# Moving the DMAs that sum w3 w_out from the end of attention into the products of the second and third pair of rows

## The chip, the cores and the metric

The kernel runs on one core of one Trainium2 chip. The metric is the device time of one execution in microseconds; lower is better. The engines are TensorE (PE in the profile, with its weight loads as PEld), VectorE (DVE), ScalarE (ACT), GpSimd (POOL) and SyncE (SP). Here SP issues the plain DMAs; POOL issues the DMAs that accumulate into their target.

## The reference

Causal attention is followed by two feed-forward blocks. All arrays are float32, and the matmuls are done on a high and a low part of each operand, in three products.

```
attn = softmax(mask(q @ k.T / 8)) @ v           # 2 batches, 12 heads, 448 tokens, 64 per head
x    = attn as (896 tokens, 768)
ab   = (x @ w1) * (x @ w2)                      # w1, w2: 768 x 1024
h    = (ab @ w3) @ w_out                        # w3: 1024 x 1024, w_out: 1024 x 768
out  = relu(h @ w_in2)**2 @ w_out2              # w_in2: 768 x 2048, w_out2: 2048 x 768
```

## The kernel before

The kernel computes W = w3 w_out during attention, in gaps between attention's own matmuls, so that h = ab W is a single matrix product. W has 1024 rows, kept as 8 blocks of 128 rows. Each finished block is stored from the tile `wraw` into the DRAM tile `w_dram` (L588; the last block by L858).

The products x w1, x w2 and ab W are done in the manner of Strassen, with seven products of sums of blocks in place of eight. The products run in the order `SEVEN = "1265734"`, and each number has its own sum of blocks on either side. For ab W, products 1, 2 and 4 read blocks of `w_dram` itself, and products 5, 6, 3 and 7 read sums of its blocks. These sums are made by DMAs alone, in the DRAM tile `s_dram`, with one group of four sums for each pair of row blocks d (0 to 3). `w_sums(d)` first copies one block four times into `s_dram[d]` with one SP DMA of 768 KB (L914), and then accumulates three other blocks with POOL DMAs (L917) of 576, 576 and 192 KB. Each of the four DMAs needs the one before it. The fourth group also needs the last block of W, which is stored at the very end of attention.

After the last matmuls of attention the work is written by hand into a list, `prog`. Each entry names its engine with a cost, what it reads and writes, and optional predecessors (`after`). `prog.order()` plays the list through with the costs and gives every engine its order. An entry given as a predecessor only in `after` places the entry in that order; it makes no wait on the chip when no data goes between the two. TensorE's order is fixed by `plan`:

- four pairs of rows d = 0 to 3, each with 14 products of 9 matmuls with 448 columns. For each number of `SEVEN`, first the product with the pair of w1 and then the one with the pair of w2 (`("w2", m)` with m = 2d) is done;
- the products of ab W, called h products here, 36 matmuls for each number. The blocks of W come in two halves, i = 0 (groups d = 0 and 1) and i = 1 (groups d = 2 and 3), and each half is one load into a slot of `xs` (L970), one cast by ScalarE into the ring and one low half by VectorE (L820);
- the last two products, with w_in2 and w_out2, up to the end.

A block of w1 or w2 comes as 768 KB into one of two `raw` buffers (L187). ScalarE (L996) and VectorE (L1000, L1004) turn it into float32; SP's next load waits until L1004 has read the buffer. ScalarE casts it into one of 8 ring slots (L827), and VectorE makes the low half there (L820). The x blocks are made in the same manner: three of B21 in `xB`, and then T2, T1, T3 and T4 in tiles named `xT`. The `xT` tiles lie in memory that attention and `wraw` have used, so the first casts into them wait until the last store of `wraw` has landed. Each of ScalarE, VectorE, POOL and SP does its instructions strictly in order.

Before the change all four calls of `w_sums` stand in `prog` without a predecessor, ahead of everything of the products:

```
    for d in range(KF // 2):
        w_sums(d)
```

Of the kernel before, what the change touches and what calls it, by code (L numbers as in the profile page):

```python
# [122 lines left out]
def attention_moe_moe2(ctx: ExitStack, tc: tile.TileContext, qk, v, w1, w2, w3, w_out, w_in2, w_out2, out):  # L123
    nc = tc.nc
    NP_ALL, P, S2 = qk.shape
    S = S2 // 2
# [8 lines left out]
    KF = w1.shape[0]  # L135
# [37 lines left out]
    def mm(o, l, r, start, stop, **more):  # L173
        return nc.tensor.matmul(o, l, r, start=start, stop=stop, **more)  # L174
# [79 lines left out]
    def wide(u):  # L254
        return u[0] in ("H", "wout2")
# [27 lines left out]
    for u in units:  # L283
# [3 lines left out]
        else:  # L287
            nm, m = key
# [459 lines left out]
    prog = Program({"A": 700, "V": 100})  # L748
# [3 lines left out]
    def act(width, psum=False, strided=False):  # L752
        gap = 60 + 0.815 * width if psum else 75 + (0.96 if strided else 0.845) * width
        return {"A": (gap, gap + 105)}

    def dve(width, fast=False):
        gap = 70 + (0.52 if fast else 1.038) * width
        return {"V": (gap, gap + 85)}
# [7 lines left out]
    def pe(columns):  # L766
        return {"T": (columns * PE_ROW, columns * PE_ROW + 170)}
# [3 lines left out]
    def bank(i):  # L771
        if i not in banks:
            pool, tag = (pools["ps"], "mm") if i < 6 else (ps_w, "w")
            banks[i] = pool.tile([P, S], F32, tag=tag, name=f"bank{i}")
        return banks[i]
# [13 lines left out]
    def slot_of_block(of, n, k):  # L789

        if of == "x":
            return "x", n, k
        if of == "h":
            return XSLOTS[H_AT[n] + k]
        if n in ("T2", "T1", "T3"):
            return XSLOTS[("T2", "T1", "T3").index(n) * (KF // 2) + k]
        return "G", 2 * k, int(n in ("B21", "B22"))

    def part_of_slot(slot, r):
        kind, n, k = slot  # L800
        if kind == "x":
            return tiles["x", n][:, r, k]
        return g_tile("ab", n)[:, r, k * S:(k + 1) * S]

    def both_parts(slot):
        return [slot + (r,) for r in "hl"]
# [12 lines left out]
    def tt(out, x, y, what):  # L819
        return lambda e: engine_of[e].tensor_tensor(out(), x(), y(), op=what)  # L820
# [5 lines left out]
    def copy(out, x):  # L826
        return lambda e: engine_of[e].copy(out(), x()) if e == "A" else engine_of[e].tensor_copy(out(), x())  # L827
# [13 lines left out]
    def fs_at(i):  # L841
        return lambda: fs[:, i]

    def bank_at(i, width=S):
        return lambda: bank(i)[:, :width]
# [57 lines left out]

    S_AT = {"5": 0, "6": 1, "3": 2, "7": 3}

    def w_sums(d):
        a21, a22 = (w_dram[d, i, :, HN:] for i in range(2))
        a11, a12 = (w_dram[d, i, :, :HN] for i in range(2))
        last_row = [("wdram",)] * (d == KF // 2 - 1)

        def spread(x, n):
            return x.unsqueeze(1).to_broadcast([P, n, HN])

        prog.add({"S": (600, 4000)}, lambda e: nc.sync.dma_start(out=s_dram[d], in_=spread(a21, 4)),  # L914
                 last_row, [("sums", d)])
        for x, n0, n1 in ((a22, 0, 3), (a11, 1, 4), (a12, 2, 3)):
            prog.add({"P": (900, 5000)}, lambda e, x=x, n0=n0, n1=n1: nc.gpsimd.dma_start(  # L917
                out=s_dram[d][:, n0:n1], in_=spread(x, n1 - n0), accum_op=ALU.add),
                last_row + [("sums", d)], [("sums", d)])

    for d in range(KF // 2):
        w_sums(d)

# [117 lines left out]
    def ring_names(u):  # L1043
        k = slot_of[u]
        return [("ring", i, s) for i in ((k, k + 1) if wide(u) else (k,)) for s in "hl"]
# [3 lines left out]
    def take_bank():  # L1049
        return free_banks.pop(0)  # L1050

    def take_fs():
        return free_fs.pop(0)

    def out_of_bank(i, n):

        prog.add(act(S, True), copy(fs_at(n), bank_at(i)), [("bank", i)], [("fs", n)])
# [56 lines left out]
    def ab_places(of, n):  # L1114

        places.update(slot_of_block(of, n, k) for k in range(KH if of == "x" else KF // 2))
        for at in [x for x in ab_later if x[0] in places]:
            ab_later.remove(at)
            at[1]()
# [16 lines left out]
    def dummy(t, i, whole):  # L1136


        def run(e):
            if whole:  # L1140
                mm(bank(i), t[0][:, :P], xB["B11"][:, 0, 0], True, True)
            else:
                x = t[0][:, :P].bitcast(F32)
                mm(bank(i)[:, HN:], x, x[:, :S - HN], False, True, skip_group_check=True)

        return run

    def product(n, pair, unit, first_of_all):


        st = state.setdefault(pair, {})
        nm, m = pair
        of, out = ("h", g_out) if nm == "win2" else ("x", ab_out)
        t = hls[unit]
        chain = CHAIN[n]
        start = chain not in st
        if start:
            st[chain] = take_bank()
        i = st[chain]
        if n == "1":  # L1160
            j = st["b"] = take_bank()
            if written[j] < S:
                prog.add(pe(S if not written[j] else 2 * (S - HN)), dummy(t, j, not written[j]),
                         ring_names(unit)[:1] + [("x", "B11", 0, "h")], [("bank", j)])
            written[j] = S
        if start:
            written[i] = S
        slots = [slot_of_block(of, B_OF[n], k) for k in range(KH)]

        def run(e):  # L1170
            o = bank(i)
            if first_of_all:
                x = t[0][:, :P].bitcast(F32)
                mm(o[:, :PAUSE], x, x[:, :PAUSE], True, True)
            for k in range(KH):
                for s, r in ((0, 0), (0, 1), (1, 0)):
                    mm(o, t[s][:, k * P:(k + 1) * P], part_of_slot(slots[k], r),
                       start and k == 0 and (s, r) == (0, 0), k == KH - 1 and (s, r) == (1, 0),
                       skip_group_check=True)

        prog.add(pe(9 * S), run, ring_names(unit) + [x for slot in slots for x in both_parts(slot)]
                 + ([] if start else [("bank", i)]), [("bank", i)])
        if n == "1":
            prog.add(act(S, True), copy(bank_at(j), bank_at(i)), [("bank", i)], [("bank", j)])
        elif n in "65":
            st[n] = take_fs()
            out_of_bank(i, st[n])
        elif n in "73":
            r = st["5" if n == "7" else "6"]
            prog.add(dve(S), tt(fs_at(r), bank_at(i), fs_at(r), ALU.add), [("bank", i), ("fs", r)], [("fs", r)])  # L1190
            out(nm, m + (n == "7"), 0, r, None)
        else:
            out(nm, m + (n == "4"), 1, None, i)
        if n in "234":
            free_banks.append(i)
        if pair == ("w2", KF - 2):
            ab_places("x", B_OF[n])

    h_state = {}

# [120 lines left out]
    for at, (kind, what, which, used) in enumerate(plan):  # L1321
        for u in used:
            need_unit(u)
        if kind == "product":
            product(what, which, used[0], at == 0)
        elif kind == "h":
            h_step(what, *which, used[0])
        else:
            o_step(*what, which, used[0])
# [52 lines left out]
```

## Time and profile before

| | us |
|---|---|
| median of three runs | 546.79 (546.46 to 547.61) |
| profiled execution | 551.16 |
| its span | 549.4 |
| TensorE busy | 534.0 (97% of the span) |
| VectorE busy | 422.0 (77%) |
| ScalarE busy | 342.0 (62%) |
| POOL busy | 138.8 (25%) |

The shares are means over stages with different limits. Times in the trace are counted from the start of the span. Attention ends, and the products of the first pair of rows begin, at about 163 us; the h products begin at about 273 us.

### The profile page before, as it was taken

What the parts mean: (1) busy time and instruction counts of PE and PEld (TensorE: products, weight loads), DVE (VectorE), ACT (ScalarE), POOL (GpSimd) and SP (SyncE); (2) the same over time, 40 slices, a digit from 0 to 9 for tenths busy, and PEclk for the clock granted to TensorE, in tenths of its full rate; (3) what the DMA queues carried; (4) which work ended last, traced back from release to release, by engine and by line L of the source; (5) the groups of instructions that cost most, each with busy time, mean ns of one, the idle gap of its engine ahead of it and who ended that gap; (6) DMA issues with size and microseconds to landing.
All of it is one profiled execution on the core that took longest, in us unless ns stands there. A gap on an engine that the chain in (4) does not pass through costs nothing.

```text
span 549.4 us, 8338 instructions
## 1 busy us (share of the span) xinstructions
PE 534.0 (97%) x2977; PEld 475.7 (87%) x2977; DVE 422.0 (77%) x892; ACT 342.0 (62%) x748; POOL 138.8 (25%) x113
## 2 busy tenths in 40 slices
PE   7899989999997999999999999999999999999997
PEld 5658777888886999999999999999999999999997
DVE  4988788877777999999975899948677768776522
ACT  5787777777766665657565578926790479047800
POOL 3477776676941200000000039200010000000100
PEclk9999999999998999999999999999999999999999
DMA  8964544486889874335444311551624062403022
GB/s 294 338 206 142 159 134 170 151 241 161 213 209 278 207 216 154 134 115 140 119 114 145 119 55 58 172 173 59 203 85 172 1 194 94 173 0 116 0 110 92
DMA packets 25673, 81.27 MB, mean 148 GB/s; under 512 B 2272, under 2 KB 11744, under 8 KB 25632
## 3 DMA queue, kind: packets, MB, share of 16 engines
q1 hardware_dynamic: 21856, 75.24, 41.1%
q0 software_dynamic: 3776, 5.51, 6.4%
q8 instruction: 23, 0.38, 0.3%
q14 instruction: 18, 0.15, 0.1%
HBM read 74.84 MB, written 14.55 MB: 163 GB/s over the span
## 4 chain that ended last, share of the span: by engine, by line
PE 87%; ACT 5%; DVE 4%; DMA 2%; issue 1%; ACTq 0%; DVEq 0%
PE bank L174 68%; PE w L174 10%; PE s L174 4%; PE x L174 3%; PE pp L499 3%; ACT p L471 2%; DMA w_dram<-wraw 2%; ACT pt L510 1%; DVE p L464 1%; DVE xs L204 1%; ACT xs L198 1%; DMA qk<-in_qk 1%; DVE p L481 0%; DVE xs L820 0%; ACT hl_wout L193 0%
## 5 line engine op out<-in xcount | busy, mean ns | idle before, releaser
L174 PE MATMUL bank<-xT,ring 128*128 128x448 f32 x630 | 133.7, 368 | 0.0
L174 PEld LDWEIGHTS bank<-xT,ring 128*128 128x128 f32 x630 | 117.9, 188 | 10.9
L827 ACT CAST ring<-xs 128x384 fp32r<-128x384 f32 (+1 forms) x142 | 80.5, 581 | 75.0 <-PE bank L174 52.3
L174 PE MATMUL bank<-ring,g 128*128 128x384 f32 x672 | 117.2, 334 | 0.0
L174 PEld LDWEIGHTS bank<-ring,g 128*128 128x128 f32 x672 | 116.7, 188 | 0.1
L820 DVE TENSOR_TENSOR ring<-xs,ring 128x384 fp32r<-128x384 f32 (+1 forms) x142 | 91.3, 659 | 26.7 <-ACT ring L827 25.5
L481 POOL TENSOR_SCALAR p<-p,st 112x448 f32<-112x448 f32 (+1 forms) x84 | 97.4, 1292 | 45.0 <-DVE st L478 16.9
L174 PE MATMUL bank<-xB,ring 128*128 128x448 f32 x489 | 105.4, 371 | 3.1 <-DVE xB L820 1.8
L174 PEld LDWEIGHTS bank<-xB,ring 128*128 128x128 f32 x489 | 92.8, 190 | 12.5 <-DVE xB L820 2.1
L471 ACT ACTIVATE p<-p,st 112x448 f32<-112x448 f32 (+1 forms) x96 | 49.7, 529 | 27.6 <-DVE st L464 27.5
L820 POOL TENSOR_TENSOR g<-fs,g 128x448 fp32r<-128x448 f32 x5 | 12.1, 2434 | 162.7 <-ACT g L827 162.7
L820 DVE TENSOR_TENSOR acc<-bank,acc 128x384 f32<-128x384 f32 x42 | 21.4, 552 | 28.5 <-PE bank L174 28.3
L464 DVE CUSTOM_DVE_ANT_0 p<-s,mask 112x448 f32<-112x448 f32 (+1 forms) x96 | 36.5, 443 | 6.8 <-PE s L174 6.8
L174 PE MATMUL w<-hl_wout,w 128*128 128x384 f32 x192 | 36.2, 340 | 0.0
L820 POOL TENSOR_TENSOR xB<-fs,xB 128x448 fp32r<-128x448 f32 x3 | 3.8, 1271 | 126.2 <-ACT xB L827 126.2
L820 DVE TENSOR_TENSOR xs<-xs 128x384 f32<-128x384 f32 x64 | 34.4, 554 | 0.3
L827 ACT COPY fs<-bank 128x448 f32<-128x448 f32 x49 | 26.1, 533 | 13.5 <-PE bank L174 12.9
L174 PEld LDWEIGHTS w<-hl_wout,w 128*128 128x128 f32 x192 | 32.9, 188 | 1.3 <-issue 0.9
L174 PE MATMUL s<-qk 64*112 64x112 f32 (+3 forms) x192 | 28.5, 436 | 4.5 <-DMA qk<-in_qk 4.4
L499 PE MATMUL pp<-ident,p 112*112 112x112 f32 x240 | 27.4, 262 | 3.5 <-DVE st L464 2.7
L499 PEld LDWEIGHTS pp<-ident,p 112*112 112x112 f32 x240 | 23.6, 133 | 7.7 <-POOL p L481 3.1
L174 PE MATMUL bank<-gab,ring 128*128 128x448 f32 x144 | 30.1, 368 | 0.0
(89 smaller groups left out, 704.4 us busy)
## 6 DMA issues: line engine op xcount, KB each, us to landing
raw_wout<-in_w_out SPq DMA_DIRECT2D x24, 768.0 KB, 4.5
raw_w<-in_w SPq DMA_DIRECT2D x16, 768.0 KB, 6.0
raw_win<-in_w_in SPq DMA_DIRECT2D x16, 768.0 KB, 4.3
raw_w<-in_w SPq DMA_DIRECT2D x16, 512.0 KB, 4.0
qk<-in_qk SPq DMA_DIRECT2D x12, 448.0 KB, 5.3
s_dram<-w_dram POOLq DMA_DIRECT2D x8, 576.0 KB, 8.5
w_dram<-wraw SPq DMA_DIRECT2D x8, 384.0 KB, 6.2
s_dram<-w_dram SPq DMA_DIRECT2D x4, 768.0 KB, 6.9
```

The source lines that it names most:

```text
L174: return nc.tensor.matmul(o, l, r, start=start, stop=stop, **more)
L198: nc.scalar.activation(y, high.bitcast(F32), AF.Prelu, scale=2.0 ** -112, alpha=-2.0 ** 32)
L204: nc.vector.scalar_tensor_tensor(y.bitcast(U32), y.bitcast(U32), 3, low, op0=ALU.logical_shift_left, op1=ALU.bitwise_or)
L464: nc.vector.tensor_tensor_reduce(e, ps[j, i], mask[:, S - (i + 1) * CP:], QS, 3.0e38, ALU.add, ALU.min, st_t[p][:, 0, j, i:i + 1],)
L471: nc.scalar.activation(e, e, AF.Exp, bias=st_t[p][:, 0, j, i:i + 1], scale=-1.0, accum_out=st_t[p][:, 1, j, i:i + 1])
L481: engine.tensor_scalar(e, e, st[:, 3, i:i + 1], None, ALU.mult)
L499: nc.tensor.transpose(x[:CP, o:o + CP], pt[:, off[i] + c * CP:off[i] + (c + 1) * CP], ident[:CP, :CP],)
L510: nc.scalar.copy(pt_t[h][:, coff[PT[gi][0]]:coff[PT[gi][0]] + o], x[:CP, :o])
L820: return lambda e: engine_of[e].tensor_tensor(out(), x(), y(), op=what)
L827: return lambda e: engine_of[e].copy(out(), x()) if e == "A" else engine_of[e].tensor_copy(out(), x())
```

## The change

`w_sums` gets a predecessor, and its four calls move from the end of attention into the function that adds a product to `prog`. Groups 0 and 1 are added behind products 1 and 4 with w2 of the second pair of rows (m = 2), groups 2 and 3 behind the same products of the third pair (m = 4). Only the SP copy has the predecessor; the POOL DMAs follow it by their data. Nothing else is changed.

```diff
-    def w_sums(d):
+    def w_sums(d, behind):
...
         prog.add({"S": (600, 4000)}, lambda e: nc.sync.dma_start(out=s_dram[d], in_=spread(a21, 4)),
-                 last_row, [("sums", d)])
+                 last_row, [("sums", d)], after=[behind])
...
-    for d in range(KF // 2):
-        w_sums(d)
...
-        prog.add(pe(9 * S), run, ring_names(unit) + [x for slot in slots for x in both_parts(slot)]
+        at = prog.add(pe(9 * S), run, ring_names(unit) + [x for slot in slots for x in both_parts(slot)]
                  + ([] if start else [("bank", i)]), [("bank", i)])
...
         if pair == ("w2", KF - 2):
             ab_places("x", B_OF[n])
+        if nm == "w2" and 0 < m < KF - 2 and n in "14":
+            w_sums(m - 2 + int(n == "4"), at)
```

## Rows read from the trace of the kernel before

**Rows 1.** The chain that ended last: start us, us, what.
```profile
162.03 8.87 DMA w_dram<-wraw
...
172.51 373.13 PE bank L174 x1918
```
**Rows 2.** TensorE's timeline, 162 to 180 us; brackets: idle time before, and what ended it.
```profile
162.81 0.47 PE L174 MATMUL bank<-xB,ring 128*128 128x448 f32 x1
...
169.93 1.30 PE L174 MATMUL bank<-xB,ring 128*128 128x448 f32 x5 [1.77 <-DVE xB L820]
172.51 3.58 PE L174 MATMUL bank<-xB,ring 128*128 128x448 f32 x9 [1.28 <-ACT bank L827]
175.94 4.29 PE L174 MATMUL bank<-xT,ring 128*128 128x448 f32 x20
```
**Rows 3.** Windows: busy us of PE, PEld, DVE, ACT, POOL; granted clock; DMA share; GB/s.
```profile
172.50:176.00 3.50, 3.49 (x10) 3.12 (x11) 3.50 (x8) 3.50 (x8) 0.81 (x1) 0.53 1.12 255
...
217.00:243.00 26.00, 26.00 (x128) 23.61 (x127) 25.84 (x50) 14.72 (x28) 0.00 (x0) 1.00 0.40 130
```
**Rows 4.** Timelines of VectorE, then of ScalarE, 168 to 178 us.
```profile
168.78 0.56 DVE L1000 TENSOR_SCALAR raw_w<-raw_w 128x768 uint32<-128x768 uint32 x1 [3.97 <-DMA raw_w<-in_w]
169.26 1.16 DVE L820 TENSOR_TENSOR xB<-fs,xB 128x448 fp32r<-128x448 f32 x2
...
176.49 1.03 DVE L820 TENSOR_TENSOR ring<-xs,ring 128x384 fp32r<-128x384 f32 x2
...
171.00 1.03 ACT L827 CAST xT<-fs 128x448 fp32r<-128x448 f32 x2 [1.28 <-DMA w_dram<-wraw]
...
171.94 0.53 ACT L827 COPY bank<-bank 128x448 f32<-128x448 f32 x1
```
**Rows 5.** DMA issues and us to landing: issued at 159.9, 162.0, 103.2, 200 to 215 us.
```profile
raw_w<-in_w SPq DMA_DIRECT2D x1, 768.0 KB, 8.9
...
w_dram<-wraw SPq DMA_DIRECT2D x1, 384.0 KB, 8.9
...
w_dram<-wraw SPq DMA_DIRECT2D x1, 384.0 KB, 2.3
...
raw_w<-in_w SPq DMA_DIRECT2D x3, 768.0 KB, 4.1
```
**Rows 6.** TensorE's timeline: starts of the second, third, fourth pair; h product 6.
```profile
194.53 7.81 PE L174 MATMUL bank<-xB,ring 128*128 128x448 f32 x37
...
220.78 7.60 PE L174 MATMUL bank<-xB,ring 128*128 128x448 f32 x36
...
246.82 7.60 PE L174 MATMUL bank<-xB,ring 128*128 128x448 f32 x36
...
287.74 11.32 PE L174 MATMUL bank<-xB,ring 128*128 128x448 f32 x54
```
**Rows 7.** The sums: POOL's triggers (ns minimum, median, maximum; starts), then the page's DMA issues.
```profile
L917 POOL DMA_DIRECT2D s_dram<-w_dram x12: 807/1270/2476, 119.3 to 195.3; - x12
...
s_dram<-w_dram POOLq DMA_DIRECT2D x8, 576.0 KB, 8.5
...
s_dram<-w_dram SPq DMA_DIRECT2D x4, 768.0 KB, 6.9
```
**Rows 8.** A load of the third pair, its first reader; landing of the load of 172.3 us.
```profile
229.01 0.33 SPq L187 DMA_DIRECT2D raw_w<-in_w  x1
...
237.93 0.90 ACT L996 ACTIVATE xs<-raw_w 128x768 f32<-128x768 f32 x1
...
raw_w<-in_w SPq DMA_DIRECT2D x1, 768.0 KB, 11.1
```
**Rows 9.** h product 6, second half: load, cast; landing of the sum issued at 163.3 us.
```profile
259.80 0.36 SPq L970 DMA_DIRECT2D xs<-s_dram  x1
...
280.93 0.84 ACT L827 CAST ring<-xs 128x768 fp32r<-128x768 f32 x1
...
s_dram<-w_dram SPq DMA_DIRECT2D x1, 768.0 KB, 16.7
```

## The prediction

> **What bounds the kernel now.** I began with the chain of waits. Its last link is one unbroken run of 1,918 TensorE matmuls from 172.51 us to 545.65 us; the link ahead of it is the store of the last row of w3 w_out, 8.87 us from issue to landing [rows 1]. So from 172.51 us on TensorE sets the end, and a microsecond taken out ahead of that point, and not lost again behind it, comes off the end. The second view is TensorE's timeline where the products begin. The first product starts at 162.81 us. TensorE then stands still 1.77 us for the low half of an x block (VectorE, L820) and 1.28 us for a bank copy (ScalarE, L827) [rows 2]. Third, the windows: after the two gaps, from 172.5 to 176 us, the granted clock is 0.53, about the lower level of 1.2 GHz, against 1.00 later [rows 3]. Nine matmuls take 175.94 - 172.51 = 3.43 us there [rows 2]; 126 matmuls of one pair of rows take 246.82 - 220.78 = 26.04 us [rows 6], so nine cost 1.86 us at the upper level, and the low clock costs 1.57 us.
>
> The sum as a check: the first pair of rows takes 194.53 - 162.81 = 31.72 us against 26.04 us for the third [rows 2, 6]. About 0.6 us of the 5.68 us are the matmuls that only the first pair has (a pause, two dummies). So some 5.1 us are lost, of which 1.77 + 1.28 + 1.57 = 4.6 us are named. That is the most that this change can give here.
>
> Fourth, what was late? VectorE stands idle 3.97 us until 168.78 us for a weight load, and only then, in its order, makes the low half that TensorE waits for. ScalarE waits 1.28 us for the store of w_dram before it casts the T2 blocks, and the bank copy of TensorE's second wait is the next thing behind these casts [rows 4]. Both landings are long: that load, issued at 159.91 us, and the store, issued at 162.03 us, take 8.9 us each, where a load of the same 768 KB takes 4.1 us between 200 and 215 us and a store 2.3 us at 103 us [rows 5]. The DMAs of the sums are what else is in flight: their last SP part goes out at 163.3 us [rows 9], their accumulating parts from 119.3 to 195.3 us [rows 7].
>
> **The change, part by part.** *Removed from the end of attention:* 4 SP DMAs of 768 KB and 12 POOL DMAs (8 of 576 KB, 4 of 192 KB). They read and write DRAM alone. What they cost there is the lengthened landing of the load and the store. Bounds for the load: as before (8.9) to undisturbed (4.1); for the store 8.9 to 2.3. Load, store and the next load still overlap, so I take neither at its best: 5 us for the load (landed at 164.9), 5.6 us for the store, the middle of its bounds (landed at 167.6).
>
> Then VectorE goes on at 164.9 instead of 168.78 us, 3.9 us earlier, and its work on the x blocks (1.7 us from the start of L1000, [rows 4]) is done by about 166.6 us, ahead of TensorE's need at 169.93 - 1.77 = 168.16: the first gap goes. ScalarE reads the same load first and has its weight item (0.9 us, [rows 8]) done by about 167 us, casts two T2 parts 167.6 to 168.6 (1.03 us) and copies the bank by 169.1 (0.53 us) [rows 4]. Without the first gap TensorE asks for that bank at 168.17 + 5 x 0.207 = 169.2 us: the second gap goes too, with little to spare, and with the gaps the low clock.
>
> What is late next is VectorE. Its two low halves for the ring at 176.49 us end at 177.52 us [rows 4]; if the later one belongs to the product after the one that starts at 175.94 us, TensorE uses it, as the third of its matmuls, at 175.94 + 1.86 + 0.41 = 178.2 us, so 0.7 us are to spare. VectorE is busy 25.84 of 26 us later [rows 3] and can hardly catch up, so TensorE gains VectorE's 3.9 us and these 0.7 us, 4.6 us, not the whole 5.1. I take 0.2 us off for edges: 4.4 us.
>
> *Added behind the second and third pair:* the same 16 DMAs. SP issues the first of each sum behind the product named as its predecessor. These products end near 198.2, 220.7, 224.5 and 246.7 us of the old time (194.53 or 220.78 plus two products of 1.86; the ends of the second and third pair) [rows 6]. SP's copy waits for nothing there, since w_dram has long landed, so no load behind it in SP's queue is held. POOL has no other work until the h products; its triggers took 0.81 to 2.48 us each [rows 7] and block nothing. The cost is contention with the weight loads. The tightest load of the third pair is issued at 229.01 and first read at 237.93 us: 8.9 us of room [rows 8] for 4.1 us of landing. With at most two sums in flight I expect 6 to 8 us, so nothing late. If that cover goes, the price is the excess over 8.9 us, up to 11.1 - 8.9 = 2.2 us a load at the longest landing that the trace shows [rows 8], as VectorE waits in order.
>
> The chain from sum to reader: the fourth sum starts at 246.7 us; by the medians 6.9 for the copy, 8.5 and 8.5 for two accumulations [rows 7], what the h products of number 6 read is there at 270.6, the rest at about 279. Its load went out at 259.80 us before and is cast at 280.93; TensorE needs it 18 matmuls (3.72 us) after the first of number 6 at 287.74, at 291.5 us [rows 6, 9]. Issued at 270.6 and landing in some 4 us, the load is there at 275: 6 us to spare. Loads of the other h products behind it in SP's queue wait with it and have as much room. If the load waits for the whole sum, it lands near 283 and holds ScalarE 2 us, still ahead of TensorE's need. I take zero.
>
> A rule that speaks against this: the Trainium skill, page "DMA: Bandwidth & Descriptors", section "SWDGE vs HWDGE vs iDMA", says that the descriptors of POOL's DMAs are written to rings in SBUF and that VectorE in its two-port mode locks GpSimd out of SBUF. By it the triggers would be slowed in the products, and the sums would come late. The trace does not bear this out: twelve triggers, many beside a busy VectorE, took 2.48 us at most [rows 7].
>
> *Order:* 600 ns of SP in the planner's account move, so a load may be planned that much later. All loads have more room; zero, with up to 0.6 us as bound.
>
> **The sum.** The profiled execution took 551.16 us (549.4 us of span); less 4.4 us gives 546.8 us with a span of 545.0. The median of the runs shown is 4.4 us below the profiled one, and I assume that they lose the same at the start of the products: 546.79 - 4.4 = **542.4 us**.
>
> **Rivals.**
> *Half of it.* The load, the next load and the store contend among themselves. For: 1.9 MB in a few microseconds; a store alone took 2.3 us, but nothing shows one beside two loads without sums. If the load lands halfway between its bounds, at 6.5 us (166.4 us), VectorE gains 2.4 us, and TensorE 2.4 us too if the spare is used up by a remaining gap: 544.4 us. Chance 0.17.
> *Given back.* Loads of the third pair land as late as the worst of before, 11.1 us [rows 8]. Two loads with 9 us of room each are then 2.2 us late, 4.4 us in all, the whole gain: 546.8 us. For: two sums are begun within 4 us of each other there. Against: in the trace so long a landing comes where more sums and two loads are in flight together. Chance 0.12.
> *Slower.* The fourth sum comes too late for the h products. At the congested 16.7 us [rows 9] for each of three steps it is ready at 246.7 + 50.1 = 296.8; with 4 us of load and 2 us for cast and low half the product starts at 302.8 instead of 291.5 us. That is 11.3 us, less 4.4: 553.7 us. It decides where three steps take over 39 us, 13 each (read by 291.5 - 6 = 285.5), and costs time on the whole from 14.5 each. Against: the medians of 6.9 and 8.5, and few DMAs after 250 us. The skill's rule named above would lead here. Chance 0.08; I add 0.05 for loads still later than in the rival before.
>
> **How the numbers follow.** Forecast 0.58 (541.7 to 543.8 us by itself: the full 5.1, or the load at 6 us), half of it 0.17, given back 0.12, slower 0.13. A measurement here tells 0.2%, 1.1 us, from no change. Faster 0.58 + 0.17 = 0.75, same 0.12, slower 0.13. The range runs from 541.5, the ceiling and a little over, to 547.5, so that it takes in the case in which all is given back; what lies above is the slower one.
>
> **What would show it.** Right: no DMA of the sums before about 190 us; the load of 159.9 us lands in 4 to 6 us and the store in 4 to 6; TensorE has no gap over 0.5 us between 162.8 and 175 us and no stretch at a clock of 0.53 there; the second pair begins near 190 us; from there on TensorE's timeline is the old one 4 to 5 us earlier, to a span near 545. Wrong: the store still lands after 168.5 us, so that the bank copy stays late; VectorE waits for a weight load (L1000) between 200 and 250 us with a TensorE gap behind it; ScalarE's cast for h product 6 waits for s_dram; or the first pair, for a reason that these rows don't show, keeps its 31.7 us.

## The result and the profile after

The kernel after takes 542.72 us (median of 4 runs, 542.34 to 542.81), the kernel before 547.20 us in the runs beside it (4 runs, 546.46 to 548.38). The ratio is 0.9915, with a 95% interval of 0.9895 to 0.9935: faster by 4.5 us, where 4.4 us and 542.4 us were forecast. The profiled execution took 542.34 us, with a span of 540.6 us.

TensorE's timeline where the products begin (start us, busy us, what it did, count; a bracket would give idle time) answers to [rows 2], and below the dots to [rows 6]:

```profile
162.46 0.47 PE L174 MATMUL bank<-xB,ring 128*128 128x448 f32 x1
162.76 0.33 PE L174 MATMUL bank<-ring 128*128 128x64 f32 x2
162.90 7.75 PE L174 MATMUL bank<-xB,ring 128*128 128x448 f32 x37
170.49 4.82 PE L174 MATMUL bank<-xT,ring 128*128 128x448 f32 x23
...
188.73 7.66 PE L174 MATMUL bank<-xB,ring 128*128 128x448 f32 x37
...
214.47 7.46 PE L174 MATMUL bank<-xB,ring 128*128 128x448 f32 x36
...
240.00 7.46 PE L174 MATMUL bank<-xB,ring 128*128 128x448 f32 x36
...
280.13 11.11 PE L174 MATMUL bank<-xB,ring 128*128 128x448 f32 x54
```

Both brackets of [rows 2] are gone. The first pair of rows takes 188.73 - 162.46 = 26.27 us, where it took 31.72 us. The second and third pair take 25.74 and 25.53 us, so nothing is given back there. The product that started at 175.94 us before starts at 170.49 us, 5.45 us earlier.

The windows (busy us of PE, PEld, DVE, ACT, POOL; granted clock; DMA share; GB/s) answer to [rows 3]:

```profile
162.50:170.50 8.00, 8.00 (x43) 7.44 (x42) 8.00 (x16) 7.75 (x17) 0.00 (x0) 1.00 0.71 232
172.50:176.00 3.50, 3.50 (x19) 3.24 (x19) 3.50 (x7) 3.08 (x8) 0.00 (x0) 1.00 0.09 24
217.00:243.00 26.00, 26.00 (x130) 24.11 (x129) 26.00 (x49) 15.03 (x30) 5.41 (x5) 1.00 1.06 262
```

The clock is 1.00 (2.4 GHz) where it was 0.53, and the DMA engines, full there before, are at 0.09. Their load stands in the third window now: 1.06 where it was 0.40, with VectorE busy all 26 us.

Next VectorE's timeline, and under the dots ScalarE's, which answer to [rows 4]:

```profile
163.81 0.57 DVE L997 TENSOR_SCALAR raw_w<-raw_w 128x768 uint32<-128x768 uint32 x1
164.28 1.17 DVE L820 TENSOR_TENSOR xB<-fs,xB 128x448 fp32r<-128x448 f32 x2
...
171.74 1.03 DVE L820 TENSOR_TENSOR ring<-xs,ring 128x384 fp32r<-128x384 f32 x2 [0.23 <-ACT ring L827]
...
166.25 1.03 ACT L827 CAST xT<-fs 128x448 fp32r<-128x448 f32 x2
167.17 0.54 ACT L827 COPY bank<-bank 128x448 f32<-128x448 f32 x1
```

VectorE starts L997 (L1000 before) at 163.81 instead of 168.78 us without waiting for the load, and its ring halves at 171.74 instead of 176.49 us, 4.75 us earlier. ScalarE has its bank copy done at 167.7 us; before it began at 171.94. The landings of the load issued at 158.89 us and the store issued at 161.12 us [rows 5], then the loads and sums issued from 190 to 250 us (median us to landing last):

```profile
raw_w<-in_w SPq DMA_DIRECT2D x1, 768.0 KB, 4.1
...
w_dram<-wraw SPq DMA_DIRECT2D x1, 384.0 KB, 2.8
...
raw_w<-in_w SPq DMA_DIRECT2D x7, 768.0 KB, 6.1
s_dram<-w_dram POOLq DMA_DIRECT2D x7, 576.0 KB, 9.1
s_dram<-w_dram SPq DMA_DIRECT2D x3, 768.0 KB, 8.7
```

### The profile page after: what moved, and what is told of

It is laid out like the page before. It is cut to its first block, busy times and chain, and to the rows that moved or that the text cites. A ratio compares the mean times of both kernels' runs of the same rounds, so it can differ in the third digit from the quotient of the medians.

```text
span 540.6 us, 8332 instructions
## 1 busy us (share of the span) xinstructions
PE 528.0 (98%) x2977; PEld 474.1 (88%) x2977; DVE 420.8 (78%) x892; ACT 341.1 (63%) x748; POOL 137.7 (25%) x113
## 4 chain that ended last, share of the span: by engine, by line
PE 88%; ACT 6%; DVE 4%; issue 1%; DMA 1%; DVEq 0%; ACTq 0%
PE bank L174 69%; PE w L174 9%; PE s L174 3%; PE x L174 3%; PE pp L499 3%; ACT p L471 2%; ACT pt L510 2%; DVE p L464 1%; ACT xs L198 1%; DVE xs L204 1%; DMA qk<-in_qk 1%; DVE p L481 0%; ACT hl_wout L193 0%; DVE wraw L590 0%; DVE xB L178 0%
## 5 line engine op out<-in xcount | busy, mean ns | idle before, releaser
L174 PE MATMUL bank<-xT,ring 128*128 128x448 f32 x630 | 132.0, 366 | 0.0
L481 POOL TENSOR_SCALAR p<-p,st 112x448 f32<-112x448 f32 (+1 forms) x84 | 96.0, 1158 | 53.1 <-ACT pt L510 20.7
L174 PE MATMUL bank<-xB,ring 128*128 128x448 f32 x489 | 102.2, 366 | 0.0
L917 POOL DMA_DIRECT2D s_dram<-w_dram x12 | 14.0, 1167 | 97.6 <-DMA s_dram<-w_dram 97.6
```

The lines of the kernel that those rows point to most:

```text
L481: engine.tensor_scalar(e, e, st[:, 3, i:i + 1], None, ALU.mult)
```

## The experiments

**Does the gain come from the traffic at the end of attention, and which part of it?** Two kernels split the change. One moves the last group alone:

```diff
...
+    for d in range(KF // 2 - 1):
+        w_sums(d, None)
...
-        if nm == "w2" and 0 < m < KF - 2 and n in "14":
-            w_sums(m - 2 + int(n == "4"), at)
+        if (nm, m, n) == ("w2", KF - 4, "4"):
+            w_sums(KF // 2 - 1, at)
```

> Only the last group of sums moves (behind product 4 of the third pair); the first three stay at the end of attention. My theory: the accumulating DMAs of the first three groups, three of them begun near 156 us, are what lengthens the landing of the weight load of 159 us and of the last store of w_dram. So both TensorE waits come back in most of their size (1.8 and 1.3 us before) with the low clock: 545.5 to 547 us. Rival, the last group's copy of 163 us is what hurts: 542.5 to 543.5 us.

Measured: 546.04 us (545.59 to 548.67, 12 runs), ratio 0.9978 (0.9955 to 1.0001). Its TensorE:

```profile
162.93 0.47 PE L174 MATMUL bank<-xB,ring 128*128 128x448 f32 x1
...
168.92 1.28 PE L174 MATMUL bank<-xB,ring 128*128 128x448 f32 x5 [0.63 <-DVE xB L820]
...
171.40 2.11 PE L174 MATMUL bank<-xB,ring 128*128 128x448 f32 x9 [1.21 <-ACT bank L827]
173.35 11.63 PE L174 MATMUL bank<-xT,ring 128*128 128x448 f32 x54
...
192.12 7.66 PE L174 MATMUL bank<-xB,ring 128*128 128x448 f32 x37
```

Both waits are there, by the same engines; load and store land in 8.2 and 8.1 us. The low clock is not there: it is 1.00 from 172.5 to 176 us. The DMA queues from 158 to 164 us (packets, MB, and the time that the packets took as a share of the 16 DMA engines; q0 is POOL's queue, q1 SP's):

```profile
q0 software_dynamic: 723, 1.06, 106.3%
q1 hardware_dynamic: 29, 0.18, 7.5%
```

The three SP copies of these groups went out at 105.7, 127.2 and 144.6 us, the last landing in 5.8 us, so what fills the engines beside the load and the store is the groups' accumulating DMAs. The other kernel leaves the last group where it was and moves the first three:

```diff
...
+    w_sums(KF // 2 - 1, None)
...
-        if nm == "w2" and 0 < m < KF - 2 and n in "14":
+        if nm == "w2" and 0 < m < KF - 2 and n in "14" and (m, n) != (KF - 4, "4"):
```

> The mirror image: the last group stays at the end of attention, begun when the last store of w_dram has landed, the first three move. My theory: load (4.1 us) and store (2.8 us) have landed before the group's copy begins, so TensorE waits for nothing and the time is that of the changed kernel, 542.4 to 543.3 us. Rival, any sum there costs: 544 to 546 us.

Measured: 542.91 us (542.75 to 544.05, 6 runs), ratio 0.9910 (0.9879 to 0.9940), landings 4.2 and 2.9 us, no gap. So the three groups whose accumulations are in flight beside the load and the store made the waits. The last group alone cost nothing where it was, with the other three moved. I had expected its copy to wait for the store's landing, but it did not; only its accumulations need that block. SP issued the copy at 163.00 us, behind the load (159.49 us) and the store (161.71 us), 1.6 us before the store landed. Whether moving the last group alone gives about a microsecond, the interval of the first kernel leaves open.

**Is anything given back in the second and third pair?** This kernel makes no sums at all, and h products 5, 6, 3 and 7 read plain blocks of `w_dram`; the rest is the kernel after.

```diff
...
-                src, names = s_dram[ds, :, S_AT[n]], [("sums", d) for d in (2 * i, 2 * i + 1)]
+                src, names = w_dram[ds, 0, :, slice(0, HN)], [("wdram",)]
...
-        if nm == "w2" and 0 < m < KF - 2 and n in "14":
-            w_sums(m - 2 + int(n == "4"), at)
```

> No sums are made at all; the h products 5, 6, 3 and 7 read plain blocks of w_dram in place of sums (this leaves part of the computation out). My theory: behind the second and third pair the sums cost nothing, since every weight load lands inside its room; the time is that of the changed kernel within 0.5 us, 542.3 to 543. Rival, a part of the gain is given back there: 541.5 us or less.

Measured: 542.85 us (542.47 to 543.34, 6 runs), ratio 0.9905 (0.9875 to 0.9935). The loads of 190 to 250 us land in 4.3 us here and in 6.1 us beside the sums, and the time is the same: the added DMAs are hidden.

**Is it traffic as such, or something of POOL's accumulating DMAs?** To the kernel after, four plain SP copies of 768 KB within DRAM are added, to a tile that nobody reads, begun at 158.3 us.

```diff
+    spare = tc.dram_tile([4, P, 4, HN], F32, name="spare")
...
+    def stand_in(c):
+        x = w_dram[KF // 2 - 1, 0, :, :HN].unsqueeze(1).to_broadcast([P, 4, HN])
+        prog.add({"S": (600, 4000)}, lambda e: nc.sync.dma_start(out=spare[c], in_=x), [], [("spare", c)])
+
+    for c in range(4):
+        stand_in(c)
```

> The changed kernel with four more plain SP copies of 768 KB from DRAM to DRAM, begun near 156 us and read by nobody. My theory, contention of transfers and nothing of POOL's queue or of accumulating: the weight load of 159 us lands in 7 us or more, TensorE's gap before 170 us comes back and with it the low clock: 544.5 to 547.5 us. Rival, it was the accumulation or POOL: 542.4 to 543.2 us.

Measured: 551.27 us (550.72 to 555.01, 11 runs), ratio 1.0074 (1.0050 to 1.0097). Landings of what is issued from 158 to 163 us:

```profile
spare<-w_dram SPq DMA_DIRECT2D x4, 768.0 KB, 8.6
raw_w<-in_w SPq DMA_DIRECT2D x2, 768.0 KB, 13.3
w_dram<-wraw SPq DMA_DIRECT2D x1, 384.0 KB, 12.7
```

Its TensorE, at the first wait:

```profile
174.85 1.49 PE L175 MATMUL bank<-xB,ring 128*128 128x448 f32 x3 [6.52 <-DVE xB L821]
```

Plain copies alone bring a wait at the same place, so neither POOL nor the accumulation is needed for one. Its size was missed (544.5 to 547.5 us expected): the copies stand ahead of the load in SP's queue, which I had not counted. The load was issued at 161.14 instead of 158.89 us and then took 12.5 us itself. In the kernel before the traffic came by POOL's queue; so this run does not tell traffic beside the load from copies ahead of it in its own queue, and whether the same bytes as plain copies in another queue would cost the same stays open. The clock is 0.50 from 172.5 to 176 us.

**How much does the price of the waits vary?** The kernel before, unchanged, as a second trace of it.

> The kernel before, unchanged, profiled once more. All theories: 546 to 548 us, ratio 1.000. In the trace the gaps of 1.8 and 1.3 us and the low clock behind them come back in about this size if they belong to the program. Open: the products of 448 columns took 0.207 us a matmul in the first trace of before and 0.203 in that of after; if that belongs to the one execution, this trace shows 0.203, and the first pair of rows takes about 31 us; if it belongs to the program, 0.207 and 31.7 us.

Measured: 546.76 us (545.76 to 551.46, 10 runs), ratio 1.0005 (0.9983 to 1.0027); the profiled execution took 546.28 us.

```profile
162.42 0.47 PE L174 MATMUL bank<-xB,ring 128*128 128x448 f32 x1
...
168.59 1.27 PE L174 MATMUL bank<-xB,ring 128*128 128x448 f32 x5 [0.80 <-DVE xB L820]
171.04 3.54 PE L174 MATMUL bank<-xB,ring 128*128 128x448 f32 x9 [1.18 <-ACT bank L827]
174.42 11.11 PE L174 MATMUL bank<-xT,ring 128*128 128x448 f32 x54
...
192.66 7.66 PE L174 MATMUL bank<-xB,ring 128*128 128x448 f32 x37
```

The waits are 0.80 and 1.18 us here, not 1.77 and 1.28. The first pair takes 30.24 us, 3.97 us more than in the kernel after, and the two profiled executions differ by 546.28 - 542.34 = 3.94 us. In this pair of traces the whole difference lies in the first pair.

**What are the waits and the low clock worth apart?** In the kernel before, 14 dummy matmuls stand ahead of the two places where TensorE waits (8 and 6), so that it has work there. In the first form they go to a bank from the kernel's own list, which changes product 2 with w1; in the second, shown here, to bank 7.

```diff
+        more = {("w1", 0, "2"): (0, 8), ("w2", 0, "2"): (6, 0)}.get((nm, m, n), (0, 0))
+        spare = 7
...
+            for _ in range(more[0]):
+                mm(bank(spare), t[0][:, :P], xB["B11"][:, 0, 0], True, True)
...
+                    for _ in range(more[1] if (k, s, r) == (1, 0, 1) else 0):
+                        mm(bank(spare), t[0][:, :P], xB["B11"][:, 0, 0], True, True)
```

> The kernel before with 14 dummy matmuls of 448 columns into a free bank, 8 ahead of the matmul at which TensorE waited 1.8 us and 6 ahead of the product at which it waited 1.3 us. The waits stay as they are, but TensorE is busy in them (14 x 0.207 = 2.9 us). My theory: the low clock behind the gaps comes from the idling, so the stretch from 172.5 to 176 us runs at 1.00 and 1.3 to 1.8 us come back: 545 to 545.7 us. Rival, the low clock has another cause: 546.5 us or more, and the clock of 0.53 stays.

> The kernel before with the 14 dummy matmuls again, now all into bank 7, which nobody reads then (in the first form the six ahead of the second wait overwrote the bank with the result of product 2 of w1). My theory: the waits stay, the low clock goes, since TensorE does not idle; the first pair takes 29.2 us of the trace instead of 30.2 to 31.7, and the time is 545.6 to 546.4 us, 0.5 to 1.5 below before. Rival, that the low clock costs nothing on its own: 546.8 us or more with a clock of 1.00.

Measured: 547.29 us (546.09 to 549.32, 12 runs), ratio 1.0003 (0.9982 to 1.0025), and 546.61 us (545.38 to 550.77, 12 runs), ratio 0.9999 (0.9975 to 1.0024). The low clock is gone in both (1.00 from 172.5 to 176 us), and no gain shows; the intervals, some 0.25% either way, could hide one of about 1 us. The weight loads (PEld) of the second form show part of the reason:

```profile
172.26 1.73 PEld L174 LDWEIGHTS bank<-xB,ring 128*128 128x128 f32 x9 [0.47 <-ACT bank L827]
174.00 1.81 PEld L174 LDWEIGHTS bank<-xT,ring 128*128 128x128 f32 x9
176.25 0.30 PEld L174 LDWEIGHTS bank<-xT,ring 128*128 128x128 f32 x2 [0.44 <-ACT ring L827]
176.84 3.34 PEld L174 LDWEIGHTS bank<-xT,ring 128*128 128x128 f32 x17 [0.30 <-DVE ring L820]
```

Those of the kernel that moves the last group alone, whose clock was 1.00 too, show the same:

```profile
175.41 0.30 PEld L174 LDWEIGHTS bank<-xT,ring 128*128 128x128 f32 x2 [0.45 <-ACT ring L827]
176.00 4.15 PEld L174 LDWEIGHTS bank<-xT,ring 128*128 128x128 f32 x21 [0.30 <-DVE ring L820]
```

In these two traces TensorE's weight loads wait about 0.75 us for the ring slot to be cast and its low half made. TensorE itself loses some 0.5 us by that: its 54 matmuls behind take 11.63 us in the kernel that moves the last group, against 11.11 us in the second trace of before. The nine matmuls behind the second gap take 174.42 - 171.04 = 3.38 us in the second trace of before, most of it at the low clock, and 173.35 - 171.40 = 1.95 us in the kernel that moves the last group, at the full one; some 0.5 us of these 1.43 us goes into the next wait. That wait does not come every time: in the first form the weight loads wait 0.20 us there, and in the form that also has the narrow matmuls (below) not at all. By time these two runs settle nothing, because 14 dummies cost 2.84 us themselves, more than the 1.98 us of waits that they fill.

**How far can the groups move?** The kernel after, with its groups behind the third and fourth pair, one pair later than in the change (`if nm == "w2" and 2 < m and n in "14": w_sums(m - 4 + int(n == "4"), at)`).

> The changed kernel with the groups begun one pair later, behind products 1 and 4 of the third and fourth pair. My theory by the chain of the changed kernel's trace (last group begun 26.4 us before the load that waits for it): the last group begins at about 261 to 265 us and its second accumulation lands at 287 to 291 us; with the load (3.6 us) and 2 us for cast and low half h product 6 gets its second half at 293 to 297 us instead of 284: 9 to 13 us of waiting on TensorE, 551 to 556 us. Rival, the h products have more cover or the plan orders other loads ahead: 542.5 to 545 us.

Measured: 554.25 us (553.55 to 555.73, 4 runs), ratio 1.0141 (1.0125 to 1.0156), as expected. SP's load for h product 6:

```profile
287.04 1.38 SPq L967 DMA_DIRECT2D xs<-s_dram  x3
```

ScalarE's cast of it:

```profile
290.38 1.81 ACT L827 CAST ring<-xs 128x768 fp32r<-128x768 f32 x2 [3.31 <-DMA xs<-s_dram]
```

TensorE:

```profile
291.27 10.29 PE L174 MATMUL bank<-xB,ring 128*128 128x448 f32 x36 [6.77 <-ACT ring L827]
```

The window behind that gap:

```profile
291.20:295.00 3.80, 3.73 (x9) 2.98 (x10) 1.92 (x2) 1.38 (x3) 0.00 (x0) 0.50 1.05 382
```

The sums are late, ScalarE's cast waits for the load, TensorE idles 6.77 us, and its 36 matmuls take 10.29 us instead of 7.46 us, since the clock is at 0.50 behind the gap. That makes 6.77 + 2.83 = 9.6 us of the 554.25 - 542.72 = 11.5 us against the kernel after; a wait of 0.88 us later and a start 0.55 us later (163.01 us) are the next in its timeline. The rival "slower" is real, one pair away.

**How much traffic do the second and third pair bear?** The kernel after makes each sum twice, the second time into a DRAM tile that nobody reads (`w_sums(m - 2 + int(n == "4"), at, s_more, "more")`).

> The changed kernel with every group of sums made a second time into a DRAM tile that nobody reads, begun behind the same products. Weight loads had 8.8 us of landing at most and 10 us of room. My theory, the cover is contention with little left: landings of 10 to 13 us, VectorE waits for two or more weight loads or the h loads wait for the doubled chain: 544.5 to 550 us. Rival, the transfers have room for more: 542.4 to 543.3 us.

Measured: 556.18 us (555.26 to 559.78, 4 runs), ratio 1.0194 (1.0167 to 1.0222): the direction expected, and more than the 550 us of the upper end. Loads issued from 205 to 235 us:

```profile
raw_w<-in_w SPq DMA_DIRECT2D x4, 768.0 KB, 14.1
```

TensorE's waits:

```profile
240.37 3.71 PE L175 MATMUL bank<-xB,ring 128*128 128x448 f32 x9 [5.30 <-ACT fs L828]
...
252.91 3.98 PE L175 MATMUL bank<-xB,ring 128*128 128x448 f32 x18 [1.53 <-ACT bank L828]
...
285.52 7.57 PE L175 MATMUL bank<-gab,ring 128*128 128x448 f32 x36 [2.49 <-ACT bank L828]
```

Ahead of the first of them ScalarE waits 7.23 us and VectorE 6.16 us, until 238.9 us, for a weight load. The rival "given back" needs more traffic than the change brings; doubled, it costs 13.5 us against the kernel after. I had priced late loads by the landings of the kernel before, up to 11.1 us; here one of them took 20.7 us.

**Why does the kernel before scatter?** The 88 executions of it timed here run from 545.3 to 551.8 us, and the 16 of the kernel after, of the one without sums and of the one whose last group stays from 542.3 to 544.1 us. In the first trace of before, matmuls of 448 columns followed each other about every 207 ns for a long stretch (the last section), in the second every 203 ns. I guessed that a narrower matmul would bring back the shorter step, and put one of 384 columns ahead of each later pair's first product (seven in all), with the kernel before and with the form with dummies.

```diff
+            if n == "1" and (nm == "w1" and m > 0 or nm == "win2" and m % 4 == 0):
+                mm(o[:, :HN], t[0][:, :P], part_of_slot(slots[0], 0)[:, :HN], True, True)
```

> The kernel before with one matmul of 384 columns ahead of the first product of each pair but the first (7 in all, 0.17 us each, overwritten at once). In the first trace of before the matmuls of 448 columns came every 206.5 ns from 163 to 351 us and every 202.6 ns behind the next matmuls of 384 columns. Theory: a matmul of another width ends the slow cadence, so it can cost 0.5 us at most in place of 3.5; median 546.3 to 547, and no run above 549 (before had several). Rival, the cadence has nothing to do with the width: runs of 548 to 551 us come as often as before.

> Both additions to the kernel before: no low clock and no lasting slow cadence, only the two waits of TensorE left. Theory: what remains over the changed kernel are the waits alone, 2.5 to 3.1 us, and the seven matmuls with 1.2 us: 546 to 547 us with a spread under 1.5 us. Rival: spread as in before, 546 to 550 us.

Measured: 548.65 us (547.04 to 551.90, 12 runs), ratio 1.0020 (0.9994 to 1.0045), and 547.52 us (546.68 to 550.88, 12 runs), ratio 0.9999 (0.9977 to 1.0021). Executions above 549 us are no rarer with the narrow matmuls (6 of 12 in the first) than without (8 of 29 beside it), and one of 550.88 us is left in the second. The guess about the width falls; what sets the step stays open.

## Why the prediction was right, step by step

**What was late.** As told: the load and the store, both beside the sums. The split shows that it takes the three groups whose accumulations are in flight by then, and the stand-in that a wait there needs no accumulation. That the fourth group would cost nothing in the old place was not seen.

**The landings.** Taken at 5 us (load) and 5.6 us (store), measured 4.1 and 2.8 us: at or near the lower bounds, 4.1 and 2.3 us. The load was also issued 1.02 us earlier (158.89 us) and had landed when VectorE came to it. The contention of load, store and next load among themselves, on which the rival "half of it" stood, is hardly there. Both landings were thus taken too long, and between the two profiled executions the gain at this point is larger than forecast: 5.45 us, which is VectorE's 4.75 us and the 0.7 us to spare, with no idle time of TensorE left in the first pair.

**The 4.4 us.** The number came out by a sum that holds for the first trace only in part. That trace had longer waits than the second, and its first pair lost 31.72 - 26.27 = 5.45 us, of which some 0.35 us (the 90 matmuls behind the waits, by 4 ns) are its longer step. The difference of the two spans is 549.4 - 540.6 = 8.8 us: 0.35 us from before the products, 5.45 us in the first pair, 3.0 us behind it, where the matmuls of before came at the longer step. The assumption that the shown runs lose what the profiled one loses was thus off by 1.5 us for the second trace, which lost 3.97 us. The median difference, 4.5 us, lies between them. The mechanism was right, VectorE's gain and the 0.7 us to spare; that the number came out to 0.1 us is partly luck, since landings taken too long made the sum too small and a profiled execution with longer waits than the second trace made it too large. VectorE's ring halves came 4.75 us earlier, of which 0.35 us stem from before the products.

**The clock.** The 1.57 us was never added to VectorE's gain, and rightly: with the clock at 1.00 and the waits still there, the ring slot held TensorE up by about 0.5 us in two traces. The low clock by itself was then worth some 0.9 us, worked out from two traces and not from a time of its own: the first pair takes 30.24 us in the second trace of before and 192.12 - 162.93 = 29.19 us in the kernel that moves the last group, and its two waits are 0.14 us shorter in all.

**Contention in the second and third pair.** Loads of 6 to 8 us forecast; median 6.1, longest 8.8 us. That one was issued at 217.84 and read at 227.87 us, so its room was 10.0 us. No engine waited for a weight load there, and leaving the sums out saves nothing. The margin is thin: the DMA share is already 1.06, and doubled sums break it.

**When the sums begin.** I let each start at the end of the product named as predecessor. The four SP copies went out at 187.29, 207.06, 211.41 and 235.28 us, 5 to 7 us before those ends: the predecessor sets the place in SP's order and makes no wait. That step was wrong to the good.

**From the last sum to its reader.** Forecast: 6.9, 8.5 and 8.5 us for three steps. Measured: 10.3, 9.3 and 6.8 us from SP's issue to the landing of the second accumulation at 261.7 us, 2.5 us longer, with a start 5 us earlier. SP's load that reads it:

```profile
261.77 0.87 SPq L967 DMA_DIRECT2D xs<-s_dram  x2
```

ScalarE's cast of that load:

```profile
273.46 0.84 ACT L827 CAST ring<-xs 128x768 fp32r<-128x768 f32 x1
```

The load landed 3.6 us later, 8 us ahead of the cast; 6 us were forecast. It did not wait for the last accumulation (issued at 262.00, landed at 267.2 us), which writes another part.

**POOL's triggers.** Group L917 (minimum, median, maximum ns; first and last start):

```profile
L917 POOL DMA_DIRECT2D s_dram<-w_dram x12: 814/1236/1540, 195.0 to 262.0; - x12
```

At 0.81 to 1.54 us, with VectorE busy 26.00 of 26 us around five of them, they are no longer than in [rows 7]. The 576 KB accumulations issued from 190 to 250 us land in 9.1 us (median), where it was 8.5. The lock-out that the Trainium skill describes ("DMA: Bandwidth & Descriptors", section "SWDGE vs HWDGE vs iDMA") does not show here; no row tells in which mode VectorE ran.

**Chances.** The likeliest case came. Of the rivals, "slower" was shown to lie one pair later and "given back" at twice the sums; "half of it" has no support left.

## What to carry to other kernels

A transfer that nobody reads for 100 us is not free because it is in the background: ask which load or store with little room is in flight beside it, and put it where every load beside it has room to spare. Cost such a move from the engine that was held up (here VectorE's start, 3.9 us by the forecast) and what is late next, not from the bottleneck engine's idle time and low clock added up. Before a sum is made against one profiled execution, compare that execution's time with the median, and look where it differs.

## What the runs showed of the hardware

- Matmuls of one form, at a granted clock of 1.00, came at one of two steady steps. The same 54 matmuls on TensorE's timeline, in the first trace of before:

```profile
228.22 11.32 PE L174 MATMUL bank<-xT,ring 128*128 128x448 f32 x54
```

  and in the second:

```profile
225.69 11.11 PE L174 MATMUL bank<-xT,ring 128*128 128x448 f32 x54
```

  From start to start of the next group they take 11.16 and 10.95 us, 206.7 and 202.8 ns each. In the first trace the step is 203 ns up to the first wait; the longer one lasted from 176 us, behind the two waits, to 350 us. In the first form with dummies it set in behind a wait of 0.32 us at 198 us, with the clock at 1.00; with the narrow matmuls added, a wait of 0.31 us at the same place did not bring it. In the kernel without sums it set in at 322 us inside an unbroken run, and lasted to 343 us. What sets it is open.
- Whether the clock falls after a wait, and how far, differs between executions with waits of much the same size: 1.77 and 1.28 us of idle time gave 0.53 from 172.5 to 176 us, 0.80 and 1.18 us gave 0.75, 0.63 and 1.21 us gave 1.00, and 0.47 and 1.30 us (with the narrow matmuls) gave 0.74.
- One 768 KB load took 4.1 us without sums beside it, 6.1 us (median) beside the moved sums, 8.2 to 8.9 us beside the accumulations at the end of attention, and up to 20.7 us where every sum was made twice. A 384 KB store took 2.3 to 2.9 us, and 8.1 to 8.9 us beside these accumulations.
